# A small copy on another engine, and the first inverse's blocks and filler, in a chunked recurrence kernel

## The chip, the core and the metric

The kernel runs on one core of one Trainium2 chip. The time is the device time of one execution in microseconds; it is measured several times, and the median is compared. The engines are TensorE (PE, with its weight loads PEld), VectorE (DVE), ScalarE (ACT), GpSimd (POOL) and SyncE (SP). Each engine executes its instructions in the order in which they stand in its own queue, and waits on semaphores for the others.

## The reference

Three steps follow each other: a recurrent attention over 768 steps with a state of 40 x 40 for each of 4 x 8 heads, a mixture of 8 experts with one expert for each token, and a dense feed-forward layer.

```python
def _attn_ref(r, k, v, w, a, b):
    B, H, S, D = r.shape                       # 4, 8, 768, 40
    state = np.zeros((B, H, D, D), dtype=np.float32)
    for t in range(S):
        y[:, :, t] = np.einsum('bhd,bhde->bhe', rt, state)
        Sa = np.einsum('bhde,bhe->bhd', state, at)
        state_decay = state * wt[:, :, None, :] - np.einsum('bhd,bhe->bhde', Sa, bt)
        state = state_decay + np.einsum('bhd,bhe->bhde', vt, kt)
    return y

def reference(**kwargs):
    attn_out = _attn_ref(**attn_kwargs)
    x = np.ascontiguousarray(attn_out.transpose(0, 2, 1, 3)).reshape(B * S, H * D)
    x = _moe_ref(x=x, **moe_kwargs)            # 3072 tokens of 320, 8 experts, hidden 1024
    return _moe2_ref(x=x, **moe2_kwargs)       # 320 -> 2048 -> 320
```

## The kernel before

The attention does not step through time. It cuts the 768 steps into chunks of 64 and treats four chunks (256 steps) of two batches as one group, so there are six groups. What belongs to a group alone, and not to the state, is made ahead of it: scaled operands (`prepare`), their products (`products`), and the inverse of the unit triangular matrix of each chunk (`inverse`). Then the group's eight slots run, one for each chunk and batch; they carry the state, and they are sequential. While one group's slots run, the next group's `prepare`, `products` and `inverse` run between them. The first group (`o.start`) has no slots before it: its inverse stands alone at the start.

`prepare` runs 24 times, four times a group. It scans the decays `w` backwards on DVE (`s`), takes the reciprocal of the scan's first column, scans forward (`q`), and multiplies `kb` by `s` and `ra` by `q`. The first column of `s` (104 partitions x 8 elements) is also kept as `s0`, which the slots of the group use later. That copy stands on ACT in line 471.

`inverse` takes 31 elimination steps over 32 x 32 blocks on DVE (lines 551 and 553), turns the result around by two DVE transposes (`ttc`, `t11`), and then builds the inverse `tt` of each 64 x 64 matrix for two halves of the group:

- `diagonal(half)` copies the four 32-row blocks of `ttc` onto the diagonal of `tt[half]`. For half 0 of the first group DVE does it, otherwise POOL.
- `zp` multiplies `tt`'s high columns (blocks 1 and 3) by `l1`, ACT copies the result to `z` (line 601), `yp` multiplies `z` by `t11`, and ACT writes it, negated, into the low corner of `tt` (line 610).
- A check (line 434, an ACT activation whose sum counts) of `l1` writes its elements into `ttc`, as a place that is not needed any more. So it has to wait until all blocks of `ttc` have been read.

`fill(x, 8)` puts 8 products of ones, 128 x 128 in bf16, into a PSUM tile whose result is overwritten; in the first group they stand ahead of `zp` and of `yp`. In the first slot of a group `pp` (line 649) multiplies by `tt`, and `sa` follows.

The instructions of DVE, ACT and POOL stand in a planned order in the attention, and PE's are ordered by a scheduler. When one piece's place in the code changes, its place in these queues changes, and so may that of neighbours. After the attention come the experts and the dense layer, whose matmuls are `ph` and `po` in line 243.

Of the kernel before, what the change touches and what calls it, by code (L numbers as in the profile page):

```python
# [14 lines left out]
ALU = mybir.AluOpType  # L15
# [273 lines left out]
class Attention:  # L289
# [148 lines left out]
    def prepare(self, o, pg):  # L438

        nc = self.nc  # L440
        nw = 2 * NCS * CW
        half, bb = divmod(pg, 2)
        p4 = slice(4 * bb, 4 * bb + 4)
        if pg == 0:
            o.s0 = self.p.tile([PP, 8, NCS], F32, name="s0", bufs=4)
            o.group, o.q, o.la, o.kbr = {}, {}, {}, {}
        if bb == 0:
            o.q[half] = self.p.tile([PP, 8, 2, CW], F32, name="q", bufs=5)
        kbs, abds = (self.kb_start, self.abd_start) if o.start else (self.kb, self.abd)
        wz, ra, kb, abd = (self.ringed(*n) for n in (("wz", self.wz), ("ra", self.ra), ("kb", kbs), ("abd", abds)))  # L450
        for q in range(2):
            r = slice(q * HQ, q * HQ + D)
            nc.sync.dma_start(wz[r], self.wP[o.bp, o.g, pg, q])
            nc.sync.dma_start(kb[r].rearrange("p a x t -> p (a x t)"), self.kbP[o.bp, o.g, pg, q])
            nc.sync.dma_start(ra[r].rearrange("p a t -> p (a t)"), self.aP[o.bp, o.g, pg, q])
        w3 = wz[:, :nw].rearrange("p (c t) -> p c t", t=CW)[:, :, 1:]
        s = self.pa.tile([PP, nw], F32, name="s", bufs=2)
        s3 = s.rearrange("p (c t) -> p c t", t=CW)
        qt = o.q[half][:, p4]
        qc = qt.rearrange("p a c t -> p (a c) t")  # L460
        if o.start:
            self.check(w3, self.pa.tile([P, 2 * NCS, C], F32, name="junk", tag="t4", bufs=3)[:PP], 1.24, self.mid)
        else:
            self.check(w3, qc[:, :, :C], 1.24, self.mid)
        nc.vector.tensor_tensor_scan(s[:, ::-1], wz[:, 1:][:, ::-1], self.d1s[:, ::-1], 0.0, ALU.mult, ALU.max)
        nc.vector.reciprocal(self.d1q.rearrange("p (c t) -> p c t", t=CW)[:, :, 0], s3[:, :, 0])
        nc.vector.tensor_tensor_scan(qt.rearrange("p a c t -> p (a c t)"), wz[:, :nw], self.d1q, 0.0, ALU.mult, ALU.max)  # L467
        for x in range(2):
            eng = nc.vector if o.start else nc.gpsimd
            eng.tensor_tensor(kb[:PP, :, x, :], kb[:PP, :, x, :], s3[:, :, 1:], op=ALU.mult)  # L470
        nc.scalar.copy(o.s0[:, p4, 2 * half:2 * half + 2], s3[:, :, 0].rearrange("p (a c) -> p a c", c=2))
        for q in range(2):
            r = slice(q * HQ, q * HQ + D)
            nc.gpsimd.tensor_tensor(abd[r, :, q * C:(q + 1) * C], ra[r], qc[r, :, :C], op=ALU.mult)  # L474
        o.group[pg] = abd.rearrange("p (a c) t -> p a c t", c=2), kb.rearrange("p (a c) x t -> p a c (x t)", c=2)
# [50 lines left out]
    def inverse(self, o):  # L526

        nc = self.nc
        l1, l2 = o.l1, o.l2
        o.tt = [self.ringed("tt", self.tt) for _ in range(2)]  # L530
        ut = self.ut0 if o.start else self.unit()
        ul = self.pa.tile([P, 32, 32], F32, name="ul", tag="t4", bufs=3)
        nc.vector.transpose(ul, l2.rearrange("p c u j -> p j (c u)"))
        yield
        for j in range(31):
            n, m = 31 - j, j + 1
            if o.start:
                if j == 0:
                    tmp = self.pa.tile([P, 1024], F32, name="tmp", tag="t4", bufs=3)
                col = ul[:, j, j + 1:]  # L540
            else:
                if j == 0:
                    bank = self.work("tmp", [P, 512], "mg")
                    tmp = bank[:, :256]
                if j in (0, 8, 16):
                    j0, j1 = j, (8, 16, 32)[j // 8]
                    part = bank[:, 256:256 + (j1 - j0) * (32 - j0)].rearrange("p (a b) -> p a b", b=32 - j0)
                    nc.scalar.copy(part, ul[:, j0:j1, j0:])
                col = part[:, j - j0, j + 1 - j0:]
            tv = tmp[:, :n * m].rearrange("p (a b) -> p a b", b=m)  # L550
            nc.vector.tensor_tensor(tv, col.unsqueeze(2).to_broadcast([P, n, m]),
                                    ut[:, j, :m].unsqueeze(1).to_broadcast([P, n, m]), op=ALU.mult)
            nc.vector.tensor_tensor(ut[:, j + 1:, :m], ut[:, j + 1:, :m], tv, op=ALU.subtract)  # L553
            if j % 2:
                yield

        lows = [slice(q * 64, q * 64 + 32) for q in range(2)]
        highs = [slice(q * 64 + 32, q * 64 + 64) for q in range(2)]

        def vacant(half):  # L560
            if not o.start:
                for lo, hi in zip(lows, highs):
                    nc.gpsimd.memset(o.tt[half][lo, :, :, hi], 0.0)

        def diagonal(half):
            for q in (1, 3, 0, 2):
                r = slice(32 * q, 32 * q + 32)
                eng = nc.vector if o.start and half == 0 else nc.gpsimd
                eng.tensor_scalar(o.tt[half][r, :, :, 32 * q:32 * q + 32], ttc[r, 2 * half:2 * half + 2], 1.0, 0.0, op0=ALU.mult, op1=ALU.add)

        vacant(0)
        ttc = self.t4("ttc")
        nc.vector.transpose(ttc.rearrange("p c u t -> p t (c u)"), ut)
        diagonal(0)
        t11 = self.t4("t11")
        nc.vector.transpose(t11.rearrange("p c u s -> p s (c u)"), ut.rearrange("p t s -> p s t"))
        yield

        pairs = [(c2, u) for u in range(8) for c2 in range(2)]
        out = lambda t, c2, q: t[c2 * 64:c2 * 64 + 32, :, q * 32:q * 32 + 32]  # L580
        heads = lambda t: t.rearrange("p (q s) -> p q s", q=2)
        wide = lambda t, c, u: t.rearrange("p c u j -> p (c u j)")[:, 32 * (8 * c + u):min(32 * (8 * c + u) + C, 1024)]
        for half in range(2):
            if half:
                vacant(1)
                diagonal(1)
                self.check(ut, ut, 0.01)
                self.check(l1.rearrange("p c u j -> p (c u) j"), ttc.rearrange("p c u t -> p (c u) t"), 0.01)
                yield
            tt = o.tt[half]  # L590
            zp = self.work("zp", [P, 8, C], "mg" if o.start or half == 0 else "w1")
            if o.start:
                self.fill(zp, 8)
            for c2, u in pairs:
                w = wide(l1, 2 * half + c2, u)
                high = heads(tt[:, c2, u])[:, :, 32:]
                nc.tensor.matmul(heads(zp[c2 * 64:c2 * 64 + w.shape[1], u]), lhsT=w, rhs=high, start=True, stop=True)
            z = self.z
            for c2 in range(2):
                for q, lo in enumerate(lows):  # L600
                    nc.scalar.copy(z[lo, c2, :, q * 32:q * 32 + 32], out(zp, c2, q))
            yp = self.work("yp", [P, 8, C], "mg" if o.start or half == 0 else "w1")
            if o.start:
                self.fill(yp, 8)
            for c2, u in pairs:
                w = wide(t11, 2 * half + c2, u)
                nc.tensor.matmul(yp[c2 * 64:c2 * 64 + w.shape[1], u], lhsT=w, rhs=z[:, c2, u, :], start=True, stop=True)
            for c2 in range(2):
                for q, (lo, hi) in enumerate(zip(lows, highs)):
                    nc.scalar.activation(tt[lo, c2, :, hi], out(yp, c2, q), AF.Copy, scale=-1.0)  # L610
            yield
# [769 lines left out]
```

## Time and profile before

| | |
|---|---|
| median of 3 runs | 1092.12 us (1089.15, 1092.12, 1092.2) |
| profiled execution | 1090.49 us |
| its span in the trace | 1088.8 us |
| mean granted clock of TensorE | 0.961 |
| busy: PE / DVE / ACT / POOL | 90% / 63% / 49% / 45% |

The span counts from the first instruction of the execution to the last; 1.69 us of the time lie around it. The engines' shares are means over stages that are limited by different engines. All times on a row are counted from the start of the span.

### The profile page before, as it was taken

What the parts mean: (1) busy time and instruction counts of PE and PEld (TensorE: products, weight loads), DVE (VectorE), ACT (ScalarE), POOL (GpSimd) and SP (SyncE); (2) the same over time, 40 slices, a digit from 0 to 9 for tenths busy, and PEclk for the clock granted to TensorE, in tenths of its full rate; (3) what the DMA queues carried; (4) which work ended last, traced back from release to release, by engine and by line L of the source; (5) the groups of instructions that cost most, each with busy time, mean ns of one, the idle gap of its engine ahead of it and who ended that gap; (6) DMA issues with size and microseconds to landing.
All of it is one profiled execution on the core that took longest, in us unless ns stands there. A gap on an engine that the chain in (4) does not pass through costs nothing. (4 is left out here: it accounts for less than half of the span.)

```text
span 1088.8 us, 24353 instructions
## 1 busy us (share of the span) xinstructions
PE 980.7 (90%) x9213; PEld 871.9 (80%) x9213; DVE 681.9 (63%) x1493; ACT 536.5 (49%) x1303; POOL 490.9 (45%) x571
## 2 busy tenths in 40 slices
PE   2669987888879998887999999999999999999997
PEld 2557776777668777776899999899898988988986
DVE  9795968868978695556899753243444444344533
ACT  4657766686677777645677544421212222222211
POOL 7766677785867645320000003524435343534332
PEclk8669999999999999898999999999999999999999
DMA  4462323333323234427999643410000000000000
GB/s 121 103 204 72 93 73 81 90 77 83 89 77 84 55 68 105 111 55 262 324 332 321 212 149 106 124 46 7 19 25 25 25 25 25 26 25 25 25 1 28
DMA packets 128320, 103.33 MB, mean 95 GB/s; under 512 B 90564, under 2 KB 111044, under 8 KB 128196
## 3 DMA queue, kind: packets, MB, share of 16 engines
q1 hardware_dynamic: 125892, 93.83, 30.1%
q0 software_dynamic: 2304, 7.87, 2.3%
q8 instruction: 75, 1.23, 0.5%
q14 instruction: 49, 0.40, 0.1%
HBM read 79.39 MB, written 22.28 MB: 93 GB/s over the span
## 5 line engine op out<-in xcount | busy, mean ns | idle before, releaser
L234 POOL TENSOR_TENSOR gl<-g,gh 128x512 fp32r<-128x512 f32 x96 | 123.6, 1290 | 216.4 <-ACT gh L233 124.8
L233 ACT ACTIVATE gh<-g 128x512 fp32r<-128x512 f32 x96 | 60.8, 633 | 251.9 <-DVE g L1268 178.2
L1267 DVE TENSOR_SCALAR g<-ph,al 128x512 f32<-128x512 f32 x96 | 72.1, 751 | 160.1 <-POOL gl L234 77.6
L243 PE MATMUL ph<-x2thi,win 128*128 128x512 f32 x480 | 159.5, 397 | 0.0
L243 PE MATMUL po<-wout,gh 128*128 128x320 f32 x768 | 139.0, 310 | 0.0
L243 PEld LDWEIGHTS po<-wout,gh 128*128 128x128 f32 x768 | 122.0, 188 | 5.6
L243 PE MATMUL ph<-x2tlo,win 128*128 128x512 f32 x288 | 114.3, 397 | 0.0
L243 PEld LDWEIGHTS ph<-x2thi,win 128*128 128x128 f32 x480 | 88.6, 188 | 14.9
L243 PE MATMUL po<-we,hh 128*128 128x320 f32 (+1 forms) x480 | 92.5, 322 | 6.8 <-ACT hh L1137 6.1
L243 PE MATMUL ph<-xthi,we 128*128 128x448 f32 (+2 forms) x360 | 97.5, 342 | 0.1
L1076 POOL TENSOR_TENSOR win<-raw,win 128x1024 fp32r<-128x1024 f32 x4 | 9.6, 2406 | 185.3 <-ACT win L1074 185.2
L243 PEld LDWEIGHTS po<-we,hh 128*128 128x128 f32 (+1 forms) x480 | 75.9, 187 | 10.7 <-ACT hh L1137 6.7
L243 PE MATMUL po<-wout,gl 128*128 128x320 f32 x384 | 82.9, 312 | 0.0
L243 PE MATMUL ph<-xtlo,we 128*128 128x448 f32 (+2 forms) x216 | 73.7, 342 | 0.9 <-DVE xtlo L276 0.9
L494 PE MATMUL lp<-kb,abd 128*128 128x128 f32 x352 | 58.2, 309 | 17.2 <-POOL abd L474 10.3
L474 POOL TENSOR_TENSOR abd<-ra,q 40x512 f32<-40x512 f32 x44 | 61.4, 1396 | 22.4 <-DVE q L467 12.3
L243 PEld LDWEIGHTS ph<-xthi,we 128*128 128x128 f32 x360 | 66.5, 195 | 3.3 <-ACT xthi L273 0.2
L1268 DVE SCALAR_TENSOR_TENSOR g<-ph,g 128x512 f32<-128x512 f32 x96 | 66.3, 691 | 3.1
L243 PEld LDWEIGHTS po<-wout,gl 128*128 128x128 f32 x384 | 64.0, 188 | 3.0
L494 PEld LDWEIGHTS lp<-kb,abd 128*128 128x128 f32 x352 | 49.1, 212 | 21.6 <-POOL abd L474 10.8
L553 DVE TENSOR_TENSOR ut<-ut,tmp 128x31 f32<-128x31 f32 (+15 forms) x186 | 62.5, 336 | 3.6
L689 PE MATMUL sa<-vg,pw 128*64 128x104 f32 x768 | 57.2, 262 | 6.8 <-issue 4.6
(217 smaller groups left out, 2241.5 us busy)
## 6 DMA issues: line engine op xcount, KB each, us to landing
raw<-in_moe_w_dram SPq DMA_DIRECT2D x16, 512.0 KB
raw<-in_moe_w_dram SPq DMA_DIRECT2D x16, 480.0 KB
kb<-in_kbP_dram SPq DMA_DIRECT2D x44, 160.0 KB
r<-in_moe_w_in_dram SPq DMA_DIRECT2D x10, 512.0 KB
r<-in_moe_w_out_dram SPq DMA_DIRECT2D x10, 512.0 KB
xs_d<-tt SPq DMA_DIRECT2D x8, 560.0 KB
raw<-in_moe_w_dram SPq DMA_DIRECT2D x16, 256.0 KB
wz<-in_wP_dram SPq DMA_DIRECT2D x48, 81.4 KB
```

Of the source, the lines that this page charges most:

```text
L233: nc.scalar.activation(hi, src, AF.Copy)
L234: return lo_eng.tensor_tensor(lo, src, f32(hi), op=ALU.subtract)
L243: return nc.tensor.matmul(out, lhsT=lhsT, rhs=rhs, start=start, stop=stop)
L474: nc.gpsimd.tensor_tensor(abd[r, :, q * C:(q + 1) * C], ra[r], qc[r, :, :C], op=ALU.mult)
L494: nc.tensor.matmul(lp[:, i], lhsT=abd[:, i, c2, :], rhs=kb[:, i, c2, :], start=True, stop=True)
L553: nc.vector.tensor_tensor(ut[:, j + 1:, :m], ut[:, j + 1:, :m], tv, op=ALU.subtract)
L689: nc.tensor.matmul(sa[q * 64:q * 64 + 64, i], lhsT=x.pw[:, i, q * C:(q + 1) * C], rhs=x.vg[:, i, q, :], start=True, stop=True)
L1076: eng.tensor_tensor(wt[:, 3 + c, cs], raw, f32(wt[:, c, cs]), op=ALU.subtract)
L1267: nc.vector.tensor_scalar(g, ph, 0.0, al[:, f:f + 1], op0=ALU.min, op1=ALU.mult)
L1268: nc.vector.scalar_tensor_tensor(g, ph, 0.0, g, op0=ALU.max, op1=ALU.add)
```

## The change

There are three edits. In `prepare` the copy of the scan's first column is made by DVE, between the reciprocal and the scan `q`, and no longer by ACT after the products with `kb`. In `diagonal`, for half 0 of the first group, blocks 1 and 3 are written by ACT, and DVE writes blocks 0 and 2 alone. In `inverse` the 8 filler products ahead of `yp` are removed for both halves of the first group; those ahead of `zp` stay.

```diff
@@ prepare
         nc.vector.reciprocal(self.d1q.rearrange("p (c t) -> p c t", t=CW)[:, :, 0], s3[:, :, 0])
+        nc.vector.tensor_copy(o.s0[:, p4, 2 * half:2 * half + 2], s3[:, :, 0].rearrange("p (a c) -> p a c", c=2))
         nc.vector.tensor_tensor_scan(qt.rearrange("p a c t -> p (a c t)"), wz[:, :nw], self.d1q, 0.0, ALU.mult, ALU.max)
         for x in range(2):
             eng = nc.vector if o.start else nc.gpsimd
             eng.tensor_tensor(kb[:PP, :, x, :], kb[:PP, :, x, :], s3[:, :, 1:], op=ALU.mult)
-        nc.scalar.copy(o.s0[:, p4, 2 * half:2 * half + 2], s3[:, :, 0].rearrange("p (a c) -> p a c", c=2))
@@ inverse, diagonal(half)
             for q in (1, 3, 0, 2):
                 r = slice(32 * q, 32 * q + 32)
-                eng = nc.vector if o.start and half == 0 else nc.gpsimd
-                eng.tensor_scalar(o.tt[half][r, :, :, 32 * q:32 * q + 32], ttc[r, 2 * half:2 * half + 2], 1.0, 0.0, op0=ALU.mult, op1=ALU.add)
+                to, src = o.tt[half][r, :, :, 32 * q:32 * q + 32], ttc[r, 2 * half:2 * half + 2]
+                if o.start and half == 0 and q % 2:
+                    nc.scalar.copy(to, src)
+                else:
+                    eng = nc.vector if o.start and half == 0 else nc.gpsimd
+                    eng.tensor_scalar(to, src, 1.0, 0.0, op0=ALU.mult, op1=ALU.add)
@@ inverse, ahead of the products of yp
             yp = self.work("yp", [P, 8, C], "mg" if o.start or half == 0 else "w1")
-            if o.start:
-                self.fill(yp, 8)
```

Two places in the queues are spoken of later. The first is ACT's queue at the end of the first inverse, before the change; `wz_107` is the decays of a later `prepare`, `ut`, `ttc` and `tt_127` belong to the first inverse, and `l`, `kbr`, `vg` and `rs` to `products` and to the first slot.

```order
L434 ACTIVATE q,checks_134<-wz_107,mid_132 104x8x64
L434 ACTIVATE ut,checks_134<-ut 128x1024
L471 COPY s_1447<-s 104x4x2
L601 COPY z_120<-zp 32x8x32 x4
L434 ACTIVATE ttc,checks_134<-l_183 128x1024
L495 COPY l_617<-lp 128x128
L496 COPY l_618<-lp 128x128
L515 COPY kbr<-bp 128x320
L679 COPY vg_410<-rp 40x4x64 x2
L681 COPY rs<-rp 104x256
L471 COPY s_1447<-s 104x4x2
L610 ACTIVATE tt_127<-yp 32x8x32 x4
```

And the same place of ACT's queue with the change:

```order
L434 ACTIVATE q,checks_134<-wz_107,mid_132 104x8x64
L570 COPY tt_127<-ttc 32x16x32 x2
L434 ACTIVATE ut,checks_134<-ut 128x1024
L605 COPY z_120<-zp 32x8x32 x4
L681 COPY vg_410<-rp 40x4x64 x2
L683 COPY rs<-rp 104x256
L495 COPY l_609<-lp 128x128
L496 COPY l_610<-lp 128x128
L515 COPY kbr<-bp 128x320
L434 ACTIVATE ttc,checks_134<-l_183 128x1024
L612 ACTIVATE tt_127<-yp 32x8x32 x4
```

The two copies of `s` are gone, two blocks of `tt_127` stand ahead of the check of `ut`, and the check that overwrites `ttc` has moved behind the copies of `l`, `kbr`, `vg` and `rs`, to just before the writing of `tt_127` from `yp`.

The second place is POOL's queue at the same time, before the change; `kb_108` and `kb_109` are two buffers of `prepare`, `tt_128` is half 1.

```order
L474 TENSOR_TENSOR abd_111<-ra_126,q 40x8x64 x2
L470 TENSOR_TENSOR kb_108<-kb_108,s 104x8x64 x2
L366 MEMSET ut 128x1024
L569 TENSOR_SCALAR tt_128<-ttc 32x16x32 x4
L470 TENSOR_TENSOR kb_109<-kb_109,s 104x8x64 x2
L367 MEMSET ut 128x32
```

With the change it reads:

```order
L474 TENSOR_TENSOR abd_111<-ra_126,q 40x8x64 x2
L471 TENSOR_TENSOR kb_108<-kb_108,s 104x8x64 x2
L366 MEMSET ut 128x1024
L471 TENSOR_TENSOR kb_109<-kb_109,s 104x8x64 x2
L573 TENSOR_SCALAR tt_128<-ttc 32x16x32 x4
L367 MEMSET ut 128x32
```

The products with `kb_109` and the four blocks of half 1 have changed places: the blocks now come second.

## Rows read from the trace of the kernel before

**Rows 1.** The page: busy time of each engine, and the chain's lines.

```profile
PE 980.7 (90%) x9213; PEld 871.9 (80%) x9213; DVE 681.9 (63%) x1493; ACT 536.5 (49%) x1303; POOL 490.9 (45%) x571
...
PE ph L243 17%; PE po L243 17%; PE tr_ps L270 1%; DVE ot L1283 0%; DVEq L1333 0%
```

**Rows 2.** Windows: stretch, length, busy PE, PEld, DVE, ACT, POOL, clock, DMA share, GB/s.

```profile
36.70:73.00 36.30, 23.62 (x120) 19.48 (x120) 33.94 (x79) 23.53 (x62) 25.60 (x34) 0.62 0.71 211
...
90.70:104.60 13.90, 13.90 (x203) 11.58 (x199) 6.51 (x12) 10.11 (x34) 11.09 (x12) 1.00 0.36 96
104.60:148.00 43.40, 38.32 (x615) 32.52 (x611) 41.40 (x114) 29.86 (x94) 27.82 (x42) 1.00 0.36 83
...
172.00:360.00 188.00, 162.38 (x2512) 136.97 (x2512) 155.80 (x433) 131.09 (x395) 139.22 (x187) 0.99 0.34 82
```

**Rows 3.** Waits, 87 to 480: waiter, releaser, us in total, times, longest.

```profile
ACT s L471 <- DVE s L465: 25.1, 13, 3.2
```

**Rows 4.** Timeline of DVE at the first inverse's end: start, us, instruction, idle before.

```profile
71.20 1.95 DVE L573 STREAM_TRANSPOSE ttc<-ut 128x1024 f32<-128x1024 f32 x1
...
74.90 4.21 DVE L569 TENSOR_SCALAR tt<-ttc 32x512 f32<-32x512 f32 x4
79.15 1.53 DVE L465 TENSOR_TENSOR_SCAN s<-wz,d1s 104x520 f32<-104x520 f32 x1
...
85.12 1.24 DVE L465 TENSOR_TENSOR_SCAN s<-wz,d1s 104x520 f32<-104x520 f32 x1 [0.36 <-POOL kb L470]
```

**Rows 5.** Timeline of ACT at the same place.

```profile
80.71 0.20 ACT L471 COPY s<-s 104x8 f32<-104x8 f32 x1 [4.69 <-DVE s L465]
80.82 1.51 ACT L601 COPY z<-zp 32x256 f32<-32x256 f32 x4
82.71 1.06 ACT L434 ACTIVATE ttc<-l 128x1024 f32<-128x1024 f32 x1 [0.37 <-POOL tt L569]
...
86.50 1.54 ACT L610 ACTIVATE tt<-yp 32x256 f32<-32x256 f32 x4
```

**Rows 6.** Timeline of POOL at the same place.

```profile
76.85 1.24 POOL L366 MEMSET ut<- 128x1024 f32 x1
78.18 4.50 POOL L569 TENSOR_SCALAR tt<-ttc 32x512 f32<-32x512 f32 x4
82.76 2.33 POOL L470 TENSOR_TENSOR kb<-kb,s 104x512 f32<-104x512 f32 x2
```

**Rows 7.** Timeline of PE at the same place and to 98 us.

```profile
77.25 1.97 PE L597 MATMUL zp<-tt,l 128*64 128x64 f32 x32 [7.29 <-DVE tt L569]
...
83.04 0.62 PE L243 MATMUL yp<-ones 128*128 128x128 bf16 x8
...
87.31 1.09 PE L649 MATMUL pp<-tt,la 128*64 128x128 f32 x16 [1.13 <-ACT tt L610]
...
97.78 0.62 PE L243 MATMUL yp<-ones 128*128 128x128 bf16 x8
```

**Rows 8.** Three small operations by line: duration min/median/max in ns.

```profile
L471 ACT COPY s<-s x24: 187/203/228, 6.4 to 321.4; 104x8 f32<-104x8 f32 x24
...
L466 DVE RECIPROCAL d1q<-s x24: 153/196/207, 5.9 to 344.5; 104x8 f32<-104x8 f32 x24
...
L956 DVE SCALAR_TENSOR_TENSOR cand<-cand,iota x12: 161/176/986, 135.2 to 479.4; 128x16 f32<-128x16 f32 x12
```

**Rows 9.** Groups of DVE by shape, 85 to 480: busy us, mean ns.

```profile
L956 DVE SCALAR_TENSOR_TENSOR cand<-cand,iota 128x16 f32<-128x16 f32 x12 | 3.8, 316 | 0.1
...
L466 DVE RECIPROCAL d1q<-s 104x8 f32<-104x8 f32 x15 | 2.9, 192 | 0.1
```

**Rows 10.** The tile `ttc`: POOL's blocks of `tt`, min/median/max in ns.

```profile
L569 POOL TENSOR_SCALAR tt<-ttc x44: 607/611/1527, 78.2 to 418.4; 32x512 f32<-32x512 f32 x44
```

**Rows 11.** Timeline of ACT in a slot: a copy `s` that waited, and what followed.

```profile
172.72 0.20 ACT L471 COPY s<-s 104x8 f32<-104x8 f32 x1 [3.16 <-DVE s L465]
...
173.15 1.52 ACT L610 ACTIVATE tt<-yp 32x256 f32<-32x256 f32 x4
```

## Prediction

> **What bounds the kernel now.** I read the page first: TensorE (PE) is busy 980.7 of 1088.8 us, and the chain that ended last is nearly all `ph` and `po`, the matmuls of the two feed-forward parts [rows 1]. All of that lies behind the attention, is untouched, and starts when the attention ends; the question is how many microseconds the attention gains or loses.
>
> So I read the attention by windows [rows 2]. From 36.7 to 73.0 VectorE (DVE) is busy 33.94 of 36.30 us with the first group's inverse: the start is bound by DVE. From 90.7 to 104.6 PE is busy 13.90 of 13.90. From 104.6 to 148.0 DVE takes 41.40 of 43.40 us (the second group's inverse beside the slots), and from 172 to 360 DVE 155.80 and PE 162.38 of 188: a chain that changes hands, with DVE the most common owner. ScalarE (ACT) is half idle, but its order is fixed by hand and one of its waits concerns us: it stands at the copy `s` of L471 for 25.1 us after 87 us, 13 times [rows 3].
>
> Then the boundary at 70 to 90 us, engine by engine. DVE makes `ttc` from 71.20, makes a second transpose, and from 74.90 writes the four blocks of `tt` half 0 in 4.21 us, before the scan `s` at 79.15 [rows 4]. The products `zp` read only the columns of blocks 1 and 3, so PE starts them at 77.25, when the first two of the four are written [rows 7]. ACT could copy `z` then, but its next instruction is L471, which waits for the scan: 4.69 us idle, until 80.71. Behind it come `z`, the check that overwrites `ttc` (82.71; it must wait for GpSimd's (POOL) last read of `ttc`), and `tt<-yp` at 86.50 [rows 5]. POOL's part is `ut` 76.85, blocks of half 1 78.18 to 82.68, `kb` 82.76 [rows 6]. PE waits 1.13 us for `tt<-yp` and starts `pp` at 87.31 [rows 7]: the first slot's start. That is the place to price.
>
> **The change part by part.**
>
> *Copies on DVE ahead of the boundary.* 24 copies move. 15 fall after 85 us [rows 9], one at about 80, so 8 before 71 us. A DVE copy of this shape is not in the trace. The nearest row is the reciprocal `L466`, the same 104x8 read of the same column on the same engine: 153/196/207 ns, never stretched; the ACT copy takes 203 [rows 8]. I take 0.20 us, plus 0.03 of gap. The bounds are 0 (a copy that falls into an idle moment) and 0.99, the longest `L956` [rows 8]. DVE is nearly full before 71, so most of the eight delay `ttc`: I take six, 6 x 0.23 = +1.4 us (two fall where DVE waits anyway). `ttc` is then ready at 73.15 + 1.4 = 74.55 instead of 73.15.
>
> *Two blocks on ACT.* They are hidden on ACT, which is idle until 74.9 before. Two blocks fewer take 2 x 1.05 = 2.1 us off DVE [rows 4], so the scan `s` starts at 79.15 + 1.4 - 2.1 = 78.45 and ends about 79.8. `zp` can start near 75.8 instead of 77.25, `z` near 77.6 instead of 80.82, `yp` about 4 us earlier. Taken alone this would bring `pp` 3 us forward.
>
> *But the stall goes elsewhere.* In the changed order ACT still has the check of `ttc` ahead of `tt<-yp`, and POOL now does `kb` of the next pair before the half-1 blocks. So: scan ends 79.8, `kb` takes 2.33 to 82.1 [rows 6], the four blocks take 4.50 as now [rows 6] to 86.6, or 4 x 0.61 = 2.45 undisturbed [rows 10] to 84.6. The check then takes 1.06 and reads its sum out, about 1.2, and `tt<-yp` starts between 85.8 and 87.8, against 86.50. The next DVE scan is released by the very end of `kb` now (85.12, after a wait for POOL) [rows 4], so it will run beside the blocks; I take the upper middle, 87.2. The first slot is late by **+0.7 us** (the bounds: -1.5, with the blocks undisturbed and the eight copies at half price, and +1.7). What is late next is `pp`, and all of the first slot.
>
> *Filler.* 16 products go. The first eight (0.62 us at 83.04) stand where PE waits for ACT afterwards: nothing. The second eight (0.62 us at 97.78) stand in the stretch where PE is full [rows 2, 7], ahead of the yp of half 1: **-0.6** (bounds 0 and -0.7).
>
> *Copies on DVE in the slots.* 15 x 0.23 = 3.4 us of DVE [rows 9]; half of it on the path (DVE has 32 us idle in 188, and PE owns part of the chain [rows 2]): **+1.6**. The lower bound is 0. The upper: each takes the mean of `L956`, 0.316 [rows 9], all on the path: 15 x 0.35 = +5.2.
>
> [...]
>
> *ACT without L471.* 25.1 us of waits disappear, but a wait counts only where ready work stood behind it. At 172.72 (3.16 us) it did: the next `tt<-yp` starts at 173.15 [rows 11]; at other places the next instruction had no data yet. I take a third, 8 us, as real delay and a quarter of that as path: **-2.0** (bounds 0 and -8). Nothing reads `s0` soon, so the copy itself was never on the path.
>
> *Order.* The other movements on POOL (two index-driven scatters, one earlier and one later) are set against each other, 0.
>
> Sum: +0.7 - 0.6 + 1.6 - 2.0 = **-0.3 us**. The profiled execution took 1090.49 (1.69 around its span); with the change 1090.2. The runs shown are 1089.15, 1092.12 and 1092.2, so the profiled one lies 1.63 below the median; set against the median it would be 1091.8. I take the middle of the two, **1091.0**.
>
> **The rivals.** Under 0.3%, 3.3 us, counts as no change here: the runs before differ by 3.05 among themselves.
>
> *A. Forecast, within 3.3 us:* each side gives and takes one or two microseconds. Price 1091.0, between 1088 and 1094. Chance 0.48.
>
> *B. Faster: ACT's waits were on the path.* The 8 us count wholly, because copies such as `tt<-yp` feed PE, which feeds DVE's next evictions; the blocks of half 1 run undisturbed, for -1.5. For it speaks that ACT stands 13 times at an instruction that nobody waits for, once 3.16 us with `tt<-yp` behind it [rows 3, 11]; against it, that DVE, not ACT, is full where it counts [rows 2], so work handed over earlier waits there. -1.5 - 0.6 + 1.6 - 8 = -8.5; with half of the relief, -4.5: 1082.5 to 1086.5, most likely about 1086. It decides once more than 5.5 of the 8 us reach the end with the rest as summed. Chance 0.29.
>
> *C. Slower: the copies are held up behind POOL.* POOL's blocks stretch from 0.611 to 1.527 [rows 10] where DVE scans run beside them, and the DVE operation `L956` takes 0.176 in the middle but 0.986 once [rows 8], with a mean of 0.316 [rows 9]: DVE and POOL hold each other up here. Each new copy stands ahead of the scan `q`, on which POOL's `abd` waits, so a held copy holds the chain twice. At 0.35 each on the path and ACT's relief worth nothing the sum is +0.7 - 0.6 + 5.2 = +5.3: 1096.3. It decides from 3.3, which is 15 copies at about 0.21 all of them on the path, with no relief. Against it: the reciprocal right before it never stretched in 24 [rows 8]. Chance 0.23.
>
> [...]
>
> *D. The change does nothing at the boundary* because the check, not `z`, holds `tt<-yp`: this is in the forecast already.
>
> **How the numbers follow.** A, B and C have 0.48, 0.29 and 0.23. The time is A's. The range runs from B's middle, 1086.0, to just short of C's price, 1095.5; it leaves out about one in ten at each end. A's own range is 1088 to 1094. Faster by over 0.3% has B's chance, slower C's, and within 0.3% A's.
>
> **What would show it.** In the changed profile: ACT idle at the boundary no more before `z` (near 77 to 78) but before the check of `ttc`; `tt<-yp` at 86 to 88, `pp` within a microsecond of 87.31 plus 0.7; the first DVE copy rows near 0.2 us; the yp of half 1 without filler; the end of the attention within 3 us of now. B is right if `pp` starts before 86 and the later slots gain steadily; C, if DVE copies show 0.4 us or more, or if `abd`'s waits for `q` grow. The forecast is wrong if the clock is granted at another level somewhere in the attention than before, or if the copies ahead of 71 us move `ttc` by more than 2 us.

## The result, and the profile after

The changed kernel is slower: 1095.45 us median of 20 runs against 1088.63 of the kernel before, ratio 1.0054 with a 95% interval of 1.0037 to 1.0072, or 5.9 us of 1088.63 (the two medians themselves lie 6.8 us apart). The forecast was no change, 1091.0 in a range of 1086.0 to 1095.5, with a chance of 0.23 for slower. The profiled execution has a span of 1096.8 us, against 1088.8 before, at a mean granted clock of 0.954.

The page's first part, after (busy time, share, instructions): nothing in it tells the loss, since every share is within a point of what it was [rows 1].

```profile
PE 982.9 (90%) x9197; PEld 876.0 (80%) x9197; DVE 683.3 (62%) x1515; ACT 536.5 (49%) x1281; POOL 495.5 (45%) x571
```

The new operation is the first place to look. The line's statistics (min/median/max in ns) and DVE's timeline after, at 37 and 56 us and at the boundary, for [rows 4]:

```profile
L467 DVE COPY s<-s x24: 121/183/2443, 5.9 to 328.2; 104x8 f32<-104x8 f32 x24
```

```profile
37.19 0.50 DVE L467 COPY s<-s 104x8 f32<-104x8 f32 x1
37.23 1.96 DVE L533 STREAM_TRANSPOSE ul<-l 128x1024 f32<-128x1024 f32 x1
39.12 2.44 DVE L467 COPY s<-s 104x8 f32<-104x8 f32 x1
39.22 2.35 DVE L551 TENSOR_TENSOR tmp<-ul,ut 128x31 f32<-128x31 f32 x1
41.62 0.20 DVE L553 TENSOR_TENSOR ut<-ut,tmp 128x31 f32<-128x31 f32 x1
...
56.28 0.66 DVE L467 COPY s<-s 104x8 f32<-104x8 f32 x1
...
73.66 1.94 DVE L577 STREAM_TRANSPOSE ttc<-ut 128x1024 f32<-128x1024 f32 x1
...
79.97 1.24 DVE L465 TENSOR_TENSOR_SCAN s<-wz,d1s 104x520 f32<-104x520 f32 x1 [1.08 <-POOL kb L471]
...
81.37 0.85 DVE L467 COPY s<-s 104x8 f32<-104x8 f32 x1
...
84.37 1.24 DVE L465 TENSOR_TENSOR_SCAN s<-wz,d1s 104x520 f32<-104x520 f32 x1 [1.00 <-POOL kb L471]
```

A copy of eight columns took 0.12 to 0.16 us where no POOL instruction ran at its start, nine times of 24, and 2.44 us once. The elimination's first product behind it reads 2.35: its record begins 0.10 us after the copy's and ends 0.01 us after it. POOL's timeline at the same places, for [rows 6]:

```profile
36.15 2.28 POOL L376 MEMSET vg<- 128x832 f32 x3
...
38.76 0.44 POOL L376 MEMSET sm<- 104x416 f32 x1
39.14 0.98 POOL L376 MEMSET pw<- 128x512 f32 x2
40.08 1.46 POOL L376 MEMSET yt<- 128x512 f32 x3
...
53.63 3.29 POOL L471 TENSOR_TENSOR kb<-kb,s 104x512 f32<-104x512 f32 x2
...
77.13 2.81 POOL L471 TENSOR_TENSOR kb<-kb,s 104x512 f32<-104x512 f32 x2
79.88 0.95 POOL L366 MEMSET ut<- 128x1024 f32 x1
80.79 3.55 POOL L471 TENSOR_TENSOR kb<-kb,s 104x512 f32<-104x512 f32 x2
84.43 4.45 POOL L573 TENSOR_SCALAR tt<-ttc 32x512 f32<-32x512 f32 x4
```

The copy of 39.12 ends at 41.56; POOL's last memset ends at 41.54. POOL had started the memset of `sm` before it, and through five more that followed without a gap the copy didn't end. The other held copies waited for less. Of the 24, eleven took 0.29 us or more; each of them ended 0.02 to 0.03 us after a POOL instruction, and nine of the eleven after the first one to end. So the copy of 56.28 ends with `kb` (56.94 against 56.92), and the copy of 37.19 ends at 37.69, although POOL's run of three memsets goes on to 38.43. Why that copy ended between two memsets and the one of 39.12 did not, no run shows. `ttc` starts 2.46 us later than before (73.66 against 71.20 in [rows 4]). At the boundary POOL does `kb` first, then the blocks, as its queue said, and ends them at 88.88 where it ended them at 82.68 [rows 6]. ACT's and PE's timelines after, for [rows 5, 7]:

```profile
79.01 1.52 ACT L605 COPY z<-zp 32x256 f32<-32x256 f32 x4 [0.41 <-PE zp L601]
...
88.91 1.06 ACT L434 ACTIVATE ttc<-l 128x1024 f32<-128x1024 f32 x1 [6.56 <-POOL tt L573]
...
89.96 1.53 ACT L612 ACTIVATE tt<-yp 32x256 f32<-32x256 f32 x4
```

```profile
81.58 1.15 PE L609 MATMUL yp<-z,t 128*64 128x64 f32 x32
86.42 0.58 PE L518 MATMUL ap<-ident,abd 104*128 104x104 f32 x4 [3.70 <-DVE la L502]
...
90.76 1.97 PE L651 MATMUL pp<-tt,la 128*64 128x128 f32 x16 [2.23 <-ACT tt L612]
...
95.79 0.26 PE L691 MATMUL sa<-vg,pw 128*64 128x104 f32 x1
```

`z` is indeed 1.8 us earlier, and ACT then stands 6.56 us at the check. `pp` starts at 90.76 instead of 87.31, 3.45 us late, and takes 1.97 instead of 1.09. The window of that moment shows why, after and then before, with the granted clock in the third column from the right:

```profile
87.10:94.00 6.90, 4.67 (x45) 4.26 (x44) 1.12 (x2) 4.52 (x12) 1.87 (x3) 0.51 0.10 27
...
87.10:94.00 6.90, 6.69 (x107) 5.87 (x107) 1.62 (x3) 4.95 (x17) 3.41 (x4) 1.00 0.30 86
```

PE had stood still for 3.70 us before 86.42. From 87.1 its granted clock was 0.51, through its second wait of 2.23 us, until 94.0.

The boundary is not all of it. The slots' matmuls `sa`, before and after, with the starts of the first and the last:

```profile
L689 PE MATMUL sa<-vg,pw x768: 252/253/436, 90.7 to 470.7; 128*64 128x104 f32 x192
...
L691 PE MATMUL sa<-vg,pw x768: 252/253/436, 95.8 to 481.3; 128*64 128x104 f32 x192
```

The first is 5.1 us late and the last 10.6, while the stretch behind them, which the change doesn't touch, came out 2.6 us shorter. One trace of each kernel therefore doesn't split the loss to the microsecond.

### The profile page after: what moved, and what is told of

Its sections match the earlier page's. It is cut to its first block, busy times and chain, and to the rows that moved or that the text cites. A ratio compares the mean times of both kernels' runs of the same rounds, so it can differ in the third digit from the quotient of the medians.

```text
span 1096.8 us, 24316 instructions
## 1 busy us (share of the span) xinstructions
PE 982.9 (90%) x9197; PEld 876.0 (80%) x9197; DVE 683.3 (62%) x1515; ACT 536.5 (49%) x1281; POOL 495.5 (45%) x571
## 4 chain that ended last, share of the span: by engine, by line
PE 50%; DMA 2%; DVE 1%; ACT 1%; issue 0%; SPq 0%; POOL 0%; DVEq 0%; ACTq 0%
PE ph L243 24%; PE po L243 24%; DMA raw<-in_moe_w_dram 2%; PE tr_ps L270 1%; DMA raw<-w_out 0%; ACT wout L1092 0%; DMA xs_d<-xr,sli 0%; POOL wout L1093 0%; DVE we L1093 0%; ACT we L1076 0%; SPq L1075 0%; DVE dec L215 0%; DVE we L1080 0%; DVE dec L216 0%; DVE we L1078 0%
## 5 line engine op out<-in xcount | busy, mean ns | idle before, releaser
L675 POOL TENSOR_SCALAR vg<-sm 40x160 f32<-40x160 f32 x96 | 34.7, 362 | 65.8 <-DVE sm L712 51.6
```

Source lines behind the costliest of these rows:

```text
L675: nc.gpsimd.tensor_scalar(self.by2(x.vg[C:PP, :, q, :D]), self.halves(self.sm[q * HQ:q * HQ + D, x.p2]), 1.0, 0.0, op0=ALU.mult, op1=ALU.add)
```

## The experiments

Each ratio is against runs of the kernel before on the same chip; the traces come from several chips. "Four of the second group" are the four copies that fall beside the first inverse, at 37 to 63 us; "the 16" belong to groups three to six.

**Each edit alone.** The copies alone (the first hunk of the diff), the blocks alone (the second), the filler alone (the third), and the changed kernel with the copies put back on ACT.

> The kernel before with the copies on DVE alone (blocks of tt on DVE, filler kept). Theory P (a DVE copy is held until POOL's running instructions end; what is lost is ttc about 2.4 us late and, behind it, the first slot): slower by 4 to 7 us, ratio 1.004 to 1.006, ttc starting at 73.0 to 74.0 instead of 71.20, and one DVE copy near 39 us of over 2 us beside POOL's memsets. Theory B (the lost time comes from ACT writing two blocks and from the check of ttc ahead of tt<-yp): within 1 us of the kernel before, ratio 0.999 to 1.001. Theory F (the missing filler costs, by the clock): the same as B here.

> The kernel before with blocks 1 and 3 of tt written by ACT alone. Theory P: zp and z earlier, tt<-yp within 1.5 us of 86.5 because the check of ttc still waits for POOL's blocks; ratio 0.997 to 1.001. Theory B: slower by 3 to 6 us, ratio 1.003 to 1.006, with tt<-yp after 88.5. Theory F: no change.

> The kernel before without the 16 filler products ahead of yp, nothing else. Theory F: slower by 1.5 to 4 us with granted clock 0.50 somewhere between 83 and 95 us, where the kernel before has 1.00. Theories P and B: ratio 0.998 to 1.001, about 0.6 us earlier at most, clock at 1.00 from 83 us.

> The changed kernel with the copies put back on ACT (blocks on ACT and no filler for yp stay). Theory P: the loss is gone, ratio 0.997 to 1.001, ttc at 71.2 to 71.6. Theory B or F: slower still, ratio 1.003 to 1.006.

Measured: copies alone 1.0070 (1.0045 to 1.0096), with the held copy again 2.446 us, `ttc` at 74.02 and `pp` at 91.27. Blocks alone 0.9980 (0.9959 to 1.0001), `tt<-yp` at 84.74. Filler alone 0.9982 (0.9962 to 1.0003), clock 1.00 from 81.5 (`lp` took 2.01 us at 79.71 and 1.08 at 85.02). Without the DVE copies 0.9999 (0.9970 to 1.0028), `tt<-yp` at 84.49. The copies are the whole loss; theories B and F fall. Each of the two other edits alone is worth between nothing and a gain of some 4 us, not told from nothing.

**Which copies.** A condition picks them:

```diff
+        dve = o.bp == 0 and o.g == 1          # e5; e6: not this; e9: not (o.bp == 0 and o.g < 2); e10: o.start
+        if dve:
+            nc.vector.tensor_copy(o.s0[...], s3[:, :, 0]...)
...
+        if not dve:
+            nc.scalar.copy(o.s0[...], s3[:, :, 0]...)
```

> The kernel before with only the second group's four copies on DVE (four of 24; they fall beside the first inverse). Theory S (start: the hold beside POOL's memsets near 39 us, and POOL's queue with kb ahead of the blocks of half 1, make nearly all of the loss): slower by 4 to 7 us, ratio 1.004 to 1.0065, pp at 90 to 92. Theory D (the loss is spread: each of the 24 copies costs its share, in the slots too): 4/24 of 7 us, about 1 us, ratio 1.000 to 1.002.

> The changed kernel with only the second group's four copies back on ACT; 20 copies stay on DVE. Theory S: ratio 0.998 to 1.002, ttc at 71.2 to 72.3, no DVE copy over 1 us. Theory D: 20/24 of the loss stays, ratio 1.004 to 1.006.

> The kernel before with only the 16 copies of groups three to six on DVE; the start is as before. Theory L (the slots lose too: each copy that is held by POOL delays the scan q, POOL's product with it and the slots of the group): slower by 3 to 8 us, ratio 1.003 to 1.007, the first slot at 90 to 91.5 us as before, and each group of slots 1 to 2 us longer. Theory S (only the start loses): ratio 0.998 to 1.0015.

> The kernel before with only the first group's four copies on DVE (one held 0.84 us by POOL, three free; POOL's queue with kb ahead of the blocks of half 1). Theory L: ratio 0.999 to 1.003 (a microsecond at the boundary and no more). Theory S': what the 20 copies cost in the run before came from these four, by POOL's changed order at the boundary: ratio 1.003 to 1.007.

> The kernel before once more, for a trace from the same chip as the two runs beside it: both theories expect 1081 to 1090 us and the first slot near 90.7.

Measured: the four alone 1.0044 (1.0024 to 1.0064), `pp` at 91.09; the changed kernel without those four 1.0072 (1.0050 to 1.0095), `ttc` at 71.31 and `pp` at 86.56; the 16 alone 1.0037 (1.0016 to 1.0058), `pp` at 87.31; the first group's four alone 1.0025 (0.9998 to 1.0051), not told from nothing; the kernel before once more ran 1088.7, with `pp` at 87.09. So theory D, that each copy costs its share, fell with e5, and theory S, that only the start loses, with e6 and e9: the four lose, and the other 16 alone lose too. The parts don't add up: 0.44 and 0.72% would make 1.2%, and all 24 together cost 0.54 to 0.70%.

That the 16 lose is not the same as that the slots become longer. In e6 `pp` is early, but PE's products take longer from 84 to 90 us (`lp` 1.96 us at 84.67 and 1.16 at 92.28, `pp` 1.97) and the first `sa` starts at 93.36. In e9, and in the kernel before on the same chip (e11), `sa` runs:

```profile
L693 PE MATMUL sa<-vg,pw x768: 249/253/436, 92.4 to 472.5; 128*64 128x104 f32 x192
...
L689 PE MATMUL sa<-vg,pw x768: 252/253/436, 90.5 to 471.0; 128*64 128x104 f32 x192
```

That is 380.1 and 380.5 us from the first to the last: this pair of traces shows 1.9 us lost ahead of the first `sa`, the rest of the 6.4 us between their spans behind the last one, and nothing in the slots, where theory L wanted 1 to 2 us in each group. Single traces vary by more than that: e7 and e16 below are one kernel, and their slots take 369.9 and 378.1 us.

**The same place, not a copy.** `s0` is made as the reciprocal of the reciprocal that stands just before, so that a DVE instruction of the same shape takes the copy's part (the planned order of the queues can change with it):

```diff
-        nc.vector.tensor_copy(o.s0[...], s3[:, :, 0]...)
+        nc.vector.reciprocal(o.s0[...], self.d1q.rearrange("p (c t) -> p c t", t=CW)[:, :, 0]...)
```

> The changed kernel with s0 made by DVE as the reciprocal of the reciprocal (same place, same shape, same engine, and not a copy). POOL's queue keeps kb ahead of the blocks of half 1. Theory H (a DVE copy is held by any POOL instruction that is running, an operation of another kind is not): all 24 take 0.15 to 0.21 us, none over 0.25, ttc at 71.5 to 72.8; ratio 0.999 to 1.003, the rest of the loss being POOL's queue. Theory D (any DVE instruction there costs): ratio 1.004 to 1.006, as the changed kernel.

> The changed kernel with reciprocals once more, on another chip. Theory H: ratio 0.996 to 1.000 again, so that with the first measurement it is decided whether it beats the kernel before. Rival: 1.000 to 1.003, the first measurement having been luck.

> The kernel before with only the second group's four s0 made by DVE, as reciprocals and not as copies; POOL's queue keeps kb ahead of the blocks of half 1, as in the run with the four copies. Theory H (POOL's hold on the copy is what costs): none over 0.25 us, ttc at 71.4 to 72.2, ratio 0.998 to 1.002. Rival O (POOL's changed order at the boundary is what costs): ratio 1.003 to 1.006, as with the four copies.

> The kernel before with the 16 s0 of groups three to six made by DVE as reciprocals. Theory H: ratio 0.997 to 1.001 (the 16 copies gave 1.0037). Rival W (it is DVE's own work and the order around it, not the hold): ratio 1.002 to 1.006.

The line's statistics in e7:

```profile
L467 DVE RECIPROCAL s<-d1q x24: 151/196/206, 6.0 to 338.1; 104x8 f32<-104x8 f32 x24
```

None is held, the longest takes 0.206 us, though 18 of the 24 start while POOL is at work. All 24: 0.9984 (0.9963 to 1.0006), and 0.9998 (0.9977 to 1.0019) on another chip: the loss is gone, although DVE still does 24 more instructions. The 16: 1.0019 (0.9998 to 1.0041), between the bands of theories H and W. But the second group's four: 1.0045 (1.0019 to 1.0071), against theory H. ACT and PE in that run, e13:

```profile
87.86 1.06 ACT L434 ACTIVATE ttc<-l 128x1024 f32<-128x1024 f32 x1
88.91 1.52 ACT L614 ACTIVATE tt<-yp 32x256 f32<-32x256 f32 x4
```

```profile
89.70 1.09 PE L653 MATMUL pp<-tt,la 128*64 128x128 f32 x16 [0.34 <-ACT tt L614]
```

`ttc` starts at 72.52, only 1.3 us late, but POOL's queue has `kb` ahead of the blocks, the check stands ahead of `tt<-yp`, DVE writes all four blocks of half 0 in 5.40 us beside POOL, and `pp` is 2.4 us late. In e16, with the same POOL queue, ACT writes two blocks and the check stands behind `tt<-yp` in its queue:

```profile
81.20 1.54 ACT L612 ACTIVATE tt<-yp 32x256 f32<-32x256 f32 x4
84.77 1.06 ACT L434 ACTIVATE ttc<-l 128x1024 f32<-128x1024 f32 x1 [2.03 <-POOL tt L573]
```

There `pp` starts at 85.33. So at the boundary both count, the hold (`ttc`) and the queues' new order (rival O); the order alone can cost as much as the hold.

How far a reciprocal stands for a copy depends on the queues. Counted in the traces up to 440 us, 411 of POOL's 413 instructions, 876 of DVE's 882 and 852 of ACT's 853 in e5 come in the same order in e13. This is the closest pair, and its ratios are the same, 1.0044 and 1.0045: what the hold itself costs there is not told from nothing by the times, and is 1.4 us of `pp` by the traces (91.09 and 89.70). Between the changed kernel and e7 or e16 only 365 of 409, 714 of 886 and 687 of 822 keep their order. That the loss is gone there is thus not shown to come from the missing hold alone.

**Without the check's wait.** In the first group the check writes into `tmp`, which nothing reads any more, instead of `ttc`; once in the changed kernel, once with the reciprocals.

```diff
-                self.check(l1.rearrange("p c u j -> p (c u) j"), ttc.rearrange("p c u t -> p (c u) t"), 0.01)
+                junk = tmp if o.start else ttc.rearrange("p c u t -> p (c u t)")
+                self.check(l1.rearrange("p c u j -> p (c u j)"), junk, 0.01)
```

> The changed kernel, but the second check writes its elements into tmp, which is dead by then, and so need not wait for POOL's blocks. ttc is still 2.4 us late. Theory Q (the boundary's own cost is the check that stands ahead of tt<-yp): tt<-yp at 83 to 85 and pp at 84 to 86 instead of 90.76; ratio 0.997 to 1.000 against the kernel before. Rival R (pp waits for something else then, or the slots are held by later work): pp moves, but the ratio stays at 1.003 to 1.006.

> The changed kernel with the reciprocal in place of the copy, and the check's elements written into tmp. If what the copies cost is only that POOL holds them (theory H), nothing is held here, and the boundary no longer waits for POOL's blocks: ratio 0.996 to 1.000, pp near 85 to 87. The rival (any DVE instruction at that place, or POOL's order, costs): ratio above 1.003.

Measured: 1.0079 (1.0057 to 1.0101) in the changed kernel, 0.9998 (0.9969 to 1.0028) with the reciprocals. Theory Q fell. R is what the trace of e8 shows, though the loss is above R's band:

```profile
82.81 1.54 ACT L613 ACTIVATE tt<-yp 32x256 f32<-32x256 f32 x4
```

```profile
87.41 0.95 PE L518 MATMUL ap<-ident,abd 104*128 104x104 f32 x4 [4.65 <-DVE la L502]
88.16 1.96 PE L494 MATMUL lp<-kb,abd 128*128 128x128 f32 x8
90.04 1.28 PE L652 MATMUL pp<-tt,la 128*64 128x128 f32 x16
```

`tt<-yp` is 7.15 us earlier than in the changed kernel and `pp` only 0.72: PE waits at `ap` for DVE's `la`, which stands behind both scans and both copies of the next group. The check was the last of two walls of nearly one height; the other is DVE's, and it stands because DVE is late.

**The slots, with a double dose.** The line of the 16 is written twice, as copies (e17) and as reciprocals (e18), on one chip.

> The kernel before with the 16 slot copies on DVE, each made twice (the same elements to the same place). Theory H (in the slots too the loss is the hold): the held time doubles, ratio 1.006 to 1.009. Rival W (the loss of the 16 is the changed order of the queues, which is there already with one copy): ratio 1.003 to 1.005. Rival N (the 16 cost nothing and the first measurement was luck): under 1.002.

> The same with reciprocals, each made twice: 6.4 us of DVE in 32 operations of 0.20 and none held. Theory H: ratio 0.998 to 1.003. Rival W: as the copies twice, 1.003 to 1.005.

Measured: copies twice 1.0050 (1.0026 to 1.0073), reciprocals twice 0.9983 (0.9963 to 1.0003). The intervals don't meet. Statistics of the two lines of each:

```profile
L469 DVE COPY s<-s x16: 117/164/799, 80.0 to 322.5; 104x8 f32<-104x8 f32 x16
...
L470 DVE COPY s<-s x16: 147/164/1089, 81.4 to 323.5; 104x8 f32<-104x8 f32 x16
```

```profile
L469 DVE RECIPROCAL s<-d1q x16: 188/196/206, 81.1 to 343.4; 104x8 f32<-104x8 f32 x16
...
L470 DVE RECIPROCAL s<-d1q x16: 171/192/204, 82.3 to 345.6; 104x8 f32<-104x8 f32 x16
```

The median reciprocal is longer than the median copy, and 32 of them show no cost; the copies, some of them held up to 1.1 us, cost. So for the 16 it is the hold, or what goes with it, and not DVE's extra work. The dose is not shown to double the loss: 1.0050 after 1.0037, where theory H wanted 1.006 at least, lies in the band of rival W, the changed order. Against W speaks e18, whose queues are near those of e17 and not the same (837 of DVE's 910 instructions keep their order).

**On POOL.** The copies stand on POOL, behind its products with `kb`.

> The changed kernel with the copies on POOL, behind its products with kb, in place of DVE. Nothing can be held on DVE by them. Theory H: no loss against the kernel before, ratio 0.997 to 1.001. Rival: POOL's queue becomes later by 24 operations and the products abd with it, ratio 1.001 to 1.004.

Measured: 1.0014 (0.9989 to 1.0039): no loss that can be told, and no gain; the value lies in the rival's band.

## Why the prediction was wrong

**The step that failed is the price of the copy**: "The nearest row is the reciprocal `L466`, the same 104x8 read of the same column on the same engine: 153/196/207 ns, never stretched", and from it 0.20 us. Shape, engine and operand were the same, and the kind of operation was not. A copy with no POOL instruction running at its start was no dearer than that (0.12 to 0.16 us), and the 15 that started beside one all lasted until one was done: the 24 of the changed kernel took from 0.121 to 2.443 us, eleven of them 0.29 or more, and the reciprocals between 0.151 and 0.206 (e7). The upper bound, 0.99 from the longest `L956`, was too low as well. Both of the forecast's own signs of being wrong came: `ttc` moved by more than 2 us (2.46), and the clock stood at another level (0.51 against 1.00 from 87.1 to 94.0). Rival C had this mechanism and a price of +5.3 us; the runs gave 5.9. It was set down as less likely than the forecast because of that same reciprocal row. That C's price came so near is in part luck: it put 5.2 on the copies in the slots and 0.7 on the first slot, and the trace has 5.1 us ahead of the first `sa`. The held copies ended 0.02 to 0.03 us after a POOL instruction, and the one of 2.44 us lasted through six memsets in a row.

**Copies ahead of the boundary**, forecast +1.4 us on `ttc`: 2.46 measured, most of it one copy beside the memsets. That these copies delay `ttc` was right, and the term was mis-sized.

**The first slot**, forecast +0.7 with +1.7 as the bound: `pp` came 3.45 us late. The place was right: the stall moved from `z` to the check of `ttc`, behind POOL's blocks. The path to it was not. The sum let `kb` wait for the scan; in the trace `kb` starts at 80.79, right behind POOL's memset `ut`, and that scan ends only at 81.21. It is the scan that waits 1.08 us for POOL's first `kb`. So POOL's queue set the time, and it stood 3.0 us later than before (memset `ut` at 79.88 against 76.85 in [rows 6]). The second `kb` then took 3.55 instead of 2.33, and `tt<-yp` started at 89.96, past the 87.8 that the sum allowed. What the sum had left out is the clock: PE went on at a granted clock of 0.51 from 87.1 to 94.0, so that the first `sa` came 5.1 us late (95.79 against 90.71 in the trace before). In e13, with the check in front and nothing held, the clock is 1.00 from 86 us (`pp` takes 1.09 us, not 1.97) and the first `sa` follows `pp` by 3.57 us, not by 5.03. And I took the check for the only wall; e8 shows DVE's `la` right behind it.

**Filler**, forecast -0.6: 0.9982 alone agrees, and isn't told from nothing.

**Copies in the slots and ACT's relief**, forecast +1.6 and -2.0, -0.4 together: the 16 copies with all the relief that belongs to them cost 0.37%, 4.0 us (1.7 to 6.3). As reciprocals, with the same relief, they cost 0.19% (-0.02 to 0.41) once, and twice over -0.17% (-0.37 to 0.03). So the relief of 2 us is neither shown nor excluded, and rival B's 8 us for the 25.1 us that ACT stood at L471 [rows 3] are not seen in any run. B's threshold was mis-summed, too: with the rest as summed, +1.7, it decides from 5.0 us of relief, not 5.5.

**Left open**: why the parts don't add up to the whole, and where the 4 us of the 16 copies arise. That the copies make the loss is shown (e1, e4), and so is it that the held ones ended with a POOL instruction, eleven of eleven; how much of the 5.9 us is the hold and how much the order of the queues that comes with a copy is not. No version tried is shown to beat the kernel before: the best intervals, of e2, e3, e7 and e18, all still hold 1.

## What to carry to other kernels

Price a new instruction by a row of the same kind of operation, not only of the same shape and engine; here, in one shape on one engine, reciprocals took at most 0.21 us and copies up to 2.44. Where none is in the trace, take the worst rows of its neighbours for the bound, and ask what GpSimd does at that moment: the run of memsets on GpSimd beside the elimination on VectorE looked harmless until a copy was set into it, which took those 2.44 us. Before work is moved off an engine where it waits, ask whether ready work stands behind that wait, and what stands behind the work on the engine that takes it: the 25.1 us that ACT stood at the copy were shown as a gain by no run, and four copies on VectorE beside the first inverse cost 0.44%. And when a copy is swapped for another operation to test a cause, compare the order of the queues first: only a pair with the same order tests the operation alone.

## What the runs showed of the hardware that was not expected

A DVE copy of 104x8 in float32 took 0.12 to 0.16 us in the nine cases of the changed kernel in which no POOL instruction ran at its start; the eleven of 0.29 us or more all ended 0.02 to 0.03 us after a POOL instruction. Beside a run of memsets one copy ended after the memset that was running at its start (0.50 us, from 37.19) and another only after six (2.44 us, from 39.12). A DVE reciprocal of the same shape took 0.15 to 0.21 us in 24 of 24 cases, 18 of them begun while POOL was at work (e7); so did the 24 of L466 in the changed kernel, 20 of them begun while POOL was at work. PE was at a granted clock of 0.51 for 6.9 us, from 87.1: it had waited 3.70 us up to 86.42, and its next wait, of 2.23 us, lies within the 6.9.
